# Loading queries and keys by group instead of by batch in an attention plus gated-MLP kernel

## Chip, cores and metric

One core of one Trainium2 chip. The time is the device time of one execution in microseconds; the median over several runs counts.

## The reference

Eight batches, 12 heads, 448 tokens, head dimension 64, all inputs float32. Attention with RMS-normed queries and keys is followed by a gated MLP with a spatial (token) projection. Cut to what matters:

```python
def rmsnorm(x, g):
    return x / np.sqrt(np.mean(x * x, axis=-1, keepdims=True) + 1e-06) * g

scores = matmul(rmsnorm(q, g_q), rmsnorm(k, g_k).T) / sqrt(64)
x = softmax(scores) @ v                       # 8 x 12 x 448 x 64
x = x.transpose(0, 2, 1, 3).reshape(8, 448, 768)
h = maximum(x @ w_in, 0)                      # 768 -> 1024
u, v = h[..., :512], h[..., 512:]
v = (v - mean(v)) / sqrt(var(v) + 1e-06)
v = einsum('ts,bsd->btd', w_spatial, v) + b_spatial[None, :, None]
out = (u * v) @ w_out                         # 512 -> 768
```

## The kernel before, in words

The work is cut into 24 **groups** of four heads: batch b holds groups 3b, 3b+1 and 3b+2, and group g of a batch takes heads g, g+3, g+6 and g+9. A group is handled as two pairs of heads, 128 partitions wide. For each group the kernel prepares q and k: squares (`squares`, on GpSimd, called POOL, or on ScalarE, called ACT), their sums over the head dimension (`reduce`, VectorE, called DVE), 1/rms by a logarithm and an exponential (`rstd`, ACT), the scaling to bf16 (`scaled`, POOL or DVE), and a transposition. The transposition is either done on TensorE (PE) with an identity (`transpose_pe`, followed by a copy on DVE) or by a DMA (`transpose_dma`, on the queue of SyncE, called SP); after a DMA the k side is scaled by `k_scale` on DVE (L345), tile kT from tile kr.

The scores of a group are computed in seven chunks of keys; a **pass** p is one chunk of both pairs, so group G covers passes 7G to 7G+6. Passes 0 to 19 run one at a time in the early loop (`expo` with 128x896, tile pse). From there on a **step** s covers passes 2s and 2s+1 with one exponential of 128x1792 (L372, tile et from tile pss); steps run from S0 = 10 to 83. When a group's exponentials are there, `weigh` multiplies them on PE with ones (the softmax sums) and with v (L394), `recip` turns the sums into reciprocals on ACT (L400, L401) and `xt_store` multiplies on DVE (L408). After a batch's three groups, `gated` queues that batch's MLP in pieces that `fill` hands to PE between the steps.

Every engine takes its instructions in the order of the program, which is written out by hand: `early(p)` lists what else is issued in pass p, and the tables EVEN, ODD and FIRST give the step in which a group's squares (sq), sums (red), rstd, scaling (sc), DMA transposition (tr), PE transposition (turn) and k scaling (ks) are issued, as offsets to the group's own place or, for the first groups, as absolute steps. Within a step `prep` sorts them by ORDER; `flush()` issues the output stores that the step before has left. `v_step` says when the parts of the next v are issued on POOL's queue, and the MLP's weights are issued there too (`load_w_in`, `load_w_sp`, `load_w_out`). Those transfers cast float32 to bf16.

q and k come in by SP's queue. Group 0 comes in small pieces (`load_first`, shared by SP and ACT). Groups 1 and 2 come together (`load_pair`: five heads from 1 and five from 7, k first). From batch 1 on, `load_part` brings one quarter of a batch's q or k (six heads, 384 or 288 KB) into one of two buffers, `qb0` and `qb1`. Batch 1 is issued at once, the others at the steps named first_q; a batch's load waits until the buffer's last batch has been scaled, and `qb1` takes the memory of the early tiles. The lines that issue v of batch 0 and order it behind group 1's scaled k are:

```python
        elif p == 3:
            rstd(1)
            scaled(1, 0, eng=dve)
            scaled(1, 1, eng=dve)
            after((1, 1))
            load_v(0, range(4))
```

Here `after` is a one-element copy on POOL that reads the scaled k of group 1.

Of the kernel before, what the change touches and what calls it, by code (L numbers as in the profile page):

```python
# [10 lines left out]
FP = mybir.dt.float32  # L11
BF = mybir.dt.bfloat16
# [7 lines left out]
def kernel(  # L20
# [21 lines left out]
    B, H, S, D = q.shape  # L42
    DM, DF = moe_w_in.shape
    DH = DF // 2
    P = 128
    NG = 3
    NCH = 7
# [8 lines left out]
    early_pools = ctx.enter_context(ExitStack())  # L56
    early_sb = ctx.enter_context(ExitStack())
    first = early_sb.enter_context(tc.tile_pool(name="first", bufs=1, side="right"))
    ps_e = early_pools.enter_context(tc.tile_pool(name="ps_e", bufs=2, space=PSUM, side="right"))
    ps_w = ctx.enter_context(tc.tile_pool(name="ps_w", bufs=4, space=PSUM))  # L60
    qb_pools = [ctx.enter_context(tc.tile_pool(name="qb0", bufs=1))]
# [12 lines left out]
    def lo_hi(x):  # L74
        lo = x[:, 0:256, :].rearrange("h (p c) d -> p h (c d)", c=4)
        hi = x[:, 256:S, :].rearrange("h (p c) d -> p h (c d)", c=3)
        return lo, hi
# [2 lines left out]
    k_g = [k[b].rearrange("(l g) s d -> g l s d", g=NG) for b in range(B)]  # L80
    raw = {}

    def load_pair(i):

        lo, hi = lo_hi((q, k)[i][0])
        t = first.tile([P, 5, NCH, D], FP, name=f"pair{i}")
        tv = t.rearrange("p h c d -> p h (c d)")
        for g in range(1, NG):
            raw[g, i] = t[:, g - 1:g + 3:NG]
        sync.dma_start(out=tv[0:64, :, 0:256], in_=lo[:, 1:6])  # L90
        sync.dma_start(out=tv[64:128, :, 0:192], in_=hi[:, 1:6])
        sync.dma_start(out=tv[64:128, :, 192:448], in_=lo[:, 7:12])
        sync.dma_start(out=tv[0:64, :, 256:448], in_=hi[:, 7:12])

    qbs = {}

# [39 lines left out]
    act.preload_act_table_set("natural_log_exp_and_others")  # L136
    load_first(0, 1, sync)
    load_first(1, 1, act)
    load_pair(1)
    load_pair(0)  # L140
    for n in range(8):
        load_part(1, *divmod(n, 4))


    ident = const.tile([P, P], BF)
# [262 lines left out]
        dve.tensor_tensor(out=xts[b][:, 2 * g + half, :], in0=pst.pop((G, half))[:, 0:S], in1=rec[G],  # L408
                          op=ALU.mult)

    def attend(G):
        for part in (-1, 0, 1):
            weigh(G, part)
            if part < 0:
                recip(G)
        for half in (0, 1):
            xt_store(G, half)

    def attend_late(G, i):

        if i < 3:
            weigh(G, i - 1)
        if i == 1:
            recip(G)
        if i > 1:
            xt_store(G, i - 2)

# [170 lines left out]
    S0 = 10  # L600


    squares(0, 0, 0, eng=act)
    squares(0, 1, 0)
    reduce(0, 0, 0)
    reduce(0, 1, 0)
    squares(0, 0, 1, eng=act)
# [17 lines left out]
        psp[p] = ps_e.tile([P, 2, 512], FP, name="pse")  # L625
        scores(psp[p], p)

    def after(key):

        t = st_pool.tile([1, 1], BF, name="one")  # L630
        pool.tensor_copy(out=t, in_=nrm[key][0:1, 0, 0, 0:1])


    def early(p):
        if p == 0:
            squares(1, 1)
            squares(2, 1)
            transpose_first(0, 1, dve)
            transpose_first(1, 1, dve)
        elif p == 1:  # L640
            squares(1, 0, eng=act)
        elif p == 2:
            reduce(1, 1)
            reduce(1, 0)
        elif p == 3:
            rstd(1)
            scaled(1, 0, eng=dve)
            scaled(1, 1, eng=dve)
            after((1, 1))
            load_v(0, range(4))  # L650
        elif p == 4:
            squares(2, 0, eng=act)
        elif p == 6:
            reduce(2, 1)
            reduce(2, 0)
        elif p == 8:
            rstd(2)
            scaled(2, 0, eng=dve)
            scaled(2, 1)
            squares(3, 0)  # L660
            squares(3, 1)
            load_w_in(1)
        elif p == 14:
            reduce(3, 0)
            reduce(3, 1)
        elif p == 16:
            rstd(3)
            scaled(3, 0, eng=dve)
            scaled(3, 1)
            squares(4, 0)  # L670
            squares(4, 1)
            load_w_in(0)
        elif p == 19:
            reduce(4, 0)
        if 10 <= p <= 13:
            attend_late(0, p - 10)
        if 15 <= p <= 18:
            attend_late(1, p - 15)
        if p in (0, 1, 2, 3, 4, 7, 8, 9, 14):
            dummies(6)  # L680

    TURN = {5: (1, 0), 6: (1, 1), 11: (2, 0), 12: (2, 1), 18: (3, 0), 19: (3, 1)}
    pass_scores(0)
    for p in range(2 * S0):
        expo(psp[p], p, 1)
        if p in TURN:
            transpose_pe(*TURN[p], dve)
        if p + 1 < 2 * S0:
            pass_scores(p + 1)
        early(p)  # L690
# [2 lines left out]

    EVEN = {"sq": (-11, -8), "red": (-9, -7), "rstd": (-6,), "sc": (-6, -5), "tr": (-5, -4), "ks": (-1,)}
    ODD = {"sq": (-9, -7), "red": (-6, -5), "rstd": (-3,), "sc": (-3, -2), "tr": (-2, -1), "ks": (2,)}
    FIRST = {4: {"red": (None, 10), "rstd": (11,), "sc": (11, 11), "turn": (12, 13)},
             5: {"sq": (11, 12), "red": (12, 13), "rstd": (14,), "sc": (14, 14), "turn": (15, 16)},
             6: {"sq": (14, 14), "red": (15, 16), "rstd": (17,), "sc": (17, 18), "tr": (18, 18), "ks": (20,)},
             7: {"sq": (16, 17), "red": (17, 18), "rstd": (19,), "sc": (19, 20), "tr": (20, 20), "ks": (23,)},
             8: {"sq": (18, 20), "red": (19, 21)},  # L700
             9: {"sq": (21, 23), "red": (22, 24)}}
    todo = {}
    for m in range(2, NGT // 2):
        for G, form in ((2 * m, EVEN), (2 * m + 1, ODD)):
            plan = {what: tuple(7 * m + o for o in os) for what, os in form.items()}
            if G in FIRST:
                plan = dict(plan if G > 7 else {}, **FIRST[G])
            for what, os in plan.items():
                for i, s in enumerate(os):
                    if s is not None:  # L710
                        todo.setdefault(s, []).append((what, G, i))
    for b in range(2, B):
        first_q = {2: S0, 3: 16}.get(b, (21 * b - 36) // 2)
        for n in range(4):
            todo.setdefault(first_q + n // 2, []).append(("ld", NG * b, n))
            todo.setdefault(first_q + 2 + (n if b % 2 == 0 and b > 2 else n // 2), []).append(("ld", NG * b, n + 4))

    ORDER = ("red", "rstd", "sc", "sq", "turn", "tr", "ks", "ld")

    def prep(s, early_act):  # L720
        for what, G, i in sorted(todo.get(s, ()), key=lambda x: (ORDER.index(x[0]), x[1:])):
            if (what == "rstd") != early_act:
                continue
            if what == "ld":
                load_part(G // NG, *divmod(i, 4))
            elif what == "turn":
                transpose_pe(G, i, dve)
            elif what == "sq":
                squares(G, i, eng=act if (G, i) in ((6, 1), (7, 1)) else None)
            elif what == "red":  # L730
                reduce(G, i)
            elif what == "rstd":
                rstd(G)
            elif what == "sc":
                scaled(G, i, eng=dve if (G, i) in ((4, 0), (5, 0)) else None)
            elif what == "tr":
                transpose_dma(G, i)
            elif what == "ks":
                k_scale(G)
# [5 lines left out]
    v_step = {}  # L745
    for s, b in gate_step.items():
        if b + 2 < B:
            v_step.update({s + 6 + i: (b + 2, [i]) for i in range(4)})
    busy = {attend_step(G) for G in range(NGT)}
    early_pools.close()  # L750
    early_sb.close()
    qb_pools.append(ctx.enter_context(tc.tile_pool(name="qb1", bufs=1, side="right", reuse_waits="tile")))
    ps_sc = ctx.enter_context(tc.tile_pool(name="ps_sc", bufs=1, space=PSUM, side="right", reuse_waits="tile"))
    pss = ps_sc.tile([P, 4, 512], FP, name="pss")
    rate = 0.0
    for s in range(S0, NST):
        scores(pss[:, 0:2], 2 * s)
        scores(pss[:, 2:4], 2 * s + 1)
        prep(s, True)
        expo(pss, 2 * s, 2)  # L760
        prep(s, False)
        flush()
        if s in v_step:
            load_v(*v_step[s])
        if s == 11:
            load_v(1, range(4))
        if s == 13:
            load_w_sp()
        if s == 21:
            load_w_out()  # L770
        if s in gate_step:
            b = gate_step[s]
            gated(b)
            nxt = min(x for x in list(gate_step) + [NST] if x > s)
            n = sum(1 for x in range(s, nxt - 1) if x not in busy)
            rate = sum(w[0] for w in work) / (n + 0.5)
        if s in busy:
            attend([G for G in range(NGT) if attend_step(G) == s][0])
            quota[0] = 0
        else:  # L780
            quota[0] = 1
            fill(rate)
# [9 lines left out]
    n = 0  # L792
# [35 lines left out]
```

## Time and profile before

| what | value |
|---|---|
| runs | 324.6, 325.19, 326.21 us; median 325.19 |
| profiled execution | 324.6 us, span of the instructions 322.8 us |
| PE matmul busy | 274.9 us (85% of the span) |
| ACT busy | 213.6 us (66%) |
| DVE busy | 199.0 us (62%) |
| POOL busy | 195.7 us (61%) |
| moved by DMA | 50.44 MB, mean 156 GB/s |
| mean granted TensorE clock | 0.963 |

A busy share is an average over stages with different limits, so the page's row of 40 slices and the waits of one stretch say more than the totals. A wait is listed as the engine and tile that waited, what released it, the total in us, how often, and the longest. In the timeline a line has its start, its duration, the engine, the line of the kernel, the operation with its tiles, how many instructions it merges, and in brackets the idle time before it with what ended it. PEld is the loading of PE's weights; SPq and POOLq are DMA issues on those queues.

### The profile page before, as it was taken

Reading aid. Unit: us, or ns where it says so; the run is one execution under the profiler, and the core shown is the slowest. Engines: PE = TensorE matmul, PEld = TensorE weight load, DVE = VectorE, ACT = ScalarE, POOL = GpSimd, SP = SyncE. Lnnn points to the kernel's source line nnn. Section 1 sums busy time; section 2 is a strip of 40 time slices with the busy share of each in tenths; the row PEclk is TensorE's granted clock in tenths of the full one; section 3 lists DMA queues with packets and bytes.
Section 4 is the critical chain, followed back from the end, with each engine's and each line's share of the span. In section 5 each row is a group of like instructions: output and inputs, shape, how many; then the busy total and the mean of one; then the engine's idle time right before and its main releaser. Section 6 shows DMA issues by size and latency. Waiting matters only on the chain.

```text
span 322.8 us, 6428 instructions
## 1 busy us (share of the span) xinstructions
PE 274.9 (85%) x2543; PEld 129.7 (40%) x2553; DVE 199.0 (62%) x342; ACT 213.6 (66%) x279; POOL 195.7 (61%) x175
## 2 busy tenths in 40 slices
PE   8528286979891999997999999979999999999994
PEld 8314132434440444443443444434443443444552
DVE  3737047498652759667676685686768754845552
ACT  2448157778880688776877878857786886674421
POOL 3215709985995669956986699559866960300300
PEclk9978778999998799999999999999999999999999
DMA  5999995968799999999999999998944296132156
GB/s 142 209 202 201 205 215 106 137 92 169 119 203 156 186 227 168 200 206 200 160 209 179 157 178 267 197 190 138 220 60 84 27 169 151 27 97 51 25 148 171
DMA packets 79744, 50.44 MB, mean 156 GB/s; under 512 B 42657, under 2 KB 76066, under 8 KB 79714
## 3 DMA queue, kind: packets, MB, share of 16 engines
q1 hardware_dynamic: 63922, 41.33, 67.4%
q0 software_dynamic: 15216, 8.27, 22.1%
q8 instruction: 20, 0.33, 0.5%
q10 hardware_dynamic: 576, 0.43, 0.5%
q14 instruction: 10, 0.08, 0.1%
HBM read 39.01 MB, written 11.01 MB: 155 GB/s over the span
## 4 chain that ended last, share of the span: by engine, by line
PE 41%; ACT 9%; DVE 8%; POOL 6%; DMA 6%; issue 2%; POOLq 0%; DVEq 0%; ACTq 0%
PE ps L547 9%; PE ps L473 8%; PE ps L513 7%; PE ps L394 6%; PE pss L365 6%; ACT et L372 6%; DMA w_out<-in_moe_w_out_dram 4%; PE ps L503 4%; DVE ms L256 3%; POOL sqt L248 2%; POOL vn L495 2%; DMA qT<-n 2%; DVE xt L408 1%; DVE s L481 1%; DVE osb L450 1%
## 5 line engine op out<-in xcount | busy, mean ns | idle before, releaser
L372 ACT ACTIVATE et<-pss 128x1792 bf16<-128x1792 f32 x74 | 122.9, 1661 | 46.5 <-PE pss L365 45.0
L256 DVE TENSOR_REDUCE ms<-sqt 128x14 f32<-128x896 f32 x46 | 49.3, 1075 | 21.8 <-POOL sqt L248 17.2
L408 DVE TENSOR_TENSOR xt<-ps,rc 128x448 bf16<-128x448 f32 x48 | 27.9, 619 | 43.8 <-ACT rc L401 43.1
L365 PE MATMUL pss<-qT,kT 64*128 64x448 bf16 x254 | 38.4, 360 | 17.4 <-DVE kT L345 9.1
L394 PE MATMUL ps<-et,vt 128*32 128x448 bf16 x768 | 43.7, 362 | 7.8 <-DMA vt<-in_v_dram 6.1
L547 PE MATMUL ps<-w_out,gt 128*128 128x384 bf16 (+1 forms) x256 | 48.6, 332 | 1.7 <-ACT rs L265 0.5
L473 PE MATMUL ps<-w_in_v,xt 128*128 128x512 bf16 (+1 forms) x182 | 47.0, 390 | 0.4
L275 POOL TENSOR_TENSOR n<-qb,rs 128x896 bf16<-128x896 f32 x18 | 30.5, 1694 | 24.8 <-ACT rs L265 24.7
L275 POOL TENSOR_TENSOR n<-kb,rs 128x896 bf16<-128x896 f32 x21 | 36.9, 1756 | 10.7 <-issue 9.9
L503 PE MATMUL ps<-xt,w_in_u 128*128 128x448 bf16 x192 | 40.1, 353 | 0.8 <-ACT vs L442 0.8
L248 POOL TENSOR_TENSOR sqt<-qb 128x896 f32<-128x896 f32 x21 | 36.1, 1719 | 0.0
L547 PEld LDWEIGHTS <-gt 128*128 128x128 bf16 (+1 forms) x256 | 24.6, 102 | 20.9 <-issue 7.3
L248 POOL TENSOR_TENSOR sqt<-kb 128x896 f32<-128x896 f32 x19 | 31.8, 1681 | 0.0
L394 PEld LDWEIGHTS <-vt 128*32 128x32 bf16 x768 | 21.2, 99 | 25.6 <-issue 9.0
L491 POOL TENSOR_SCALAR nm<-mv 128x4 f32<-128x4 f32 x8 | 1.8, 221 | 48.1 <-DVE mv L482 48.1
L365 PEld LDWEIGHTS <-kT 64*128 64x128 bf16 x276 | 10.8, 94 | 48.3 <-issue 28.9
L450 DVE COPY osb<-ps 128x384 f32<-128x384 f32 (+1 forms) x45 | 24.1, 555 | 9.6 <-PE ps L547 8.9
L495 POOL TENSOR_SCALAR vn<-vs,nm,rv 128x512 bf16<-128x512 bf16 (+1 forms) x32 | 24.2, 767 | 6.7 <-ACT rv L490 4.2
L513 PE MATMUL ps<-w_spT,vn 128*128 128x448 bf16 (+1 forms) x128 | 27.2, 353 | 0.1
L473 PEld LDWEIGHTS <-xt 128*128 128x128 bf16 (+1 forms) x192 | 18.2, 102 | 19.7 <-issue 5.5
L345 DVE TENSOR_SCALAR_CACHE_REDUCE kT<-kr,g_col 128x896 bf16<-128x896 bf16 x18 | 20.4, 1136 | 8.9 <-DMA kr<-n 8.9
L503 PEld LDWEIGHTS <-w_in_u 128*128 128x128 bf16 x192 | 17.3, 98 | 20.8 <-issue 7.1
(88 smaller groups left out, 336.6 us busy)
## 6 DMA issues: line engine op xcount, KB each, us to landing
out_dram<-osb SPq DMA_DIRECT2D x55, 192.0 KB, 4.3
qb<-in_q_dram SPq DMA_DIRECT2D x14, 384.0 KB, 7.0
kb<-in_k_dram SPq DMA_DIRECT2D x14, 384.0 KB, 8.7
qb<-in_q_dram SPq DMA_DIRECT2D x14, 288.0 KB, 8.3
kb<-in_k_dram SPq DMA_DIRECT2D x14, 288.0 KB, 9.6
vt<-in_v_dram POOLq DMA_DIRECT2D x16, 192.0 KB, 5.7
vt<-in_v_dram POOLq DMA_DIRECT2D x16, 144.0 KB, 5.6
w_in_v<-in_moe_w_in_dram POOLq DMA_DIRECT2D x4, 192.0 KB, 12.8
```

Of the source, the lines that this page charges most:

```text
L248: pool.tensor_tensor(out=t, in0=x, in1=x, op=ALU.mult)
L256: dve.tensor_reduce(out=sqs[gk][:, key[1], :], in_=sqt.pop(key).rearrange("p h c d -> p (h c) d"), axis=AX.X, op=ALU.add)
L275: (eng or pool).tensor_tensor(out=t.rearrange("p c h d -> p h c d"), in0=raw[key], in1=rst[gk][:, key[1], :].rearrange("p (h c) -> p h c", ...
L365: pe.matmul(out=ps[:, h, 0:S], lhsT=kT[r, c0:c0 + 128], rhs=qT[r, :], start=True, stop=True, tile_position=(64 * h, 0))
L372: act.activation(out=ets[s][:, 2 * a:2 * a + 2 * m, :], in_=ps[:, 0:2 * m, 0:S], func=AF.Exp, bias=0.0, scale=1.0)
L394: pe.matmul(out=ps[32 * l:32 * l + 32, 0:S], lhsT=w, rhs=et_of(G, 3 if r == 3 else r + 4 * y, h), start=(r == 0), stop=(r == 3), tile_posi ...
L408: dve.tensor_tensor(out=xts[b][:, 2 * g + half, :], in0=pst.pop((G, half))[:, 0:S], in1=rec[G], op=ALU.mult)
L473: pe.matmul(out=ps[0:m, :], lhsT=xts[b][:, j, t0:t0 + m], rhs=w_in_v[:, j, :], start=(j == 0), stop=(j == 5), tile_position=(0, 0))
L495: pool.tensor_scalar(out=vn_t[b % 2][0:m, c, :], in0=vs[b][c][0:m, :], scalar1=nms[b][0:m, c:c + 1], scalar2=rvs[b][0:m, c:c + 1], op0=ALU ...
L503: pe.matmul(out=ps[:, 0:S], lhsT=w_in_u[:, j, 128 * f:128 * f + 128], rhs=xts[b][:, j, :], start=(j == 0), stop=(j == 5))
L513: pe.matmul(out=ps[:, 0:S], lhsT=vn_t[b % 2][0:kp, c, 128 * f:128 * f + 128], rhs=w_spT[0:kp, c, :], start=(c == 0), stop=(c == NT - 1))
L547: pe.matmul(out=ps[o:o + m, 0:384], lhsT=gts[b][f][:, t0:t0 + m], rhs=w_out[:, f, r], start=(f == 0), stop=(f == 3), tile_position=(0, o))
```

## The change

Groups 1 to 8 (batches 0, 1 and 2) are loaded one group at a time into a pool of three buffers each for q and k; from batch 3 on the loads stay by batch. k of group 1 is issued on POOL's queue. The issues of v and of the MLP's weights move to other passes and steps, and the helper `after` goes. Groups 4 and 5 are transposed by DMA instead of on PE, group 3's transposition on PE moves behind the early loop, and the squares and scalings that ACT and DVE did for groups 4 to 7 go to POOL. `attend_late` is replaced by an `attend` that takes parts. The step tables of groups 4 to 9, first_q and v_step are changed, and the early memory is released at step 24 instead of step 10. `flush()`, `recip` and everything in the MLP stay.

The short description of the changed version reads: output stores issued in the next step, behind that step's loads and transposes; reciprocal computed in place; that of the version before: first batch loaded in three transfer sets, others a batch at a time. The stores by `flush()` in the next step and the reciprocal in place (`recip`) are in both.

```diff
+    qk_pool = early_sb.enter_context(tc.tile_pool(name="qk", bufs=3, side="right"))
...
-    def load_pair(i):
...
+    def load(G, i, eng=sync):
+        b, g = divmod(G, NG)
+        lo, hi = lo_hi((q_g, k_g)[i][b][g])
+        t = qk_pool.tile([P, 2, NCH, D], FP, name="kf" if i else "qf")
         tv = t.rearrange("p h c d -> p h (c d)")
...
+        raw[G, i] = t
+        eng.dma_start(out=tv[0:64, :, 0:256], in_=lo[:, 0:2])
+        eng.dma_start(out=tv[64:128, :, 0:192], in_=hi[:, 0:2])
+        eng.dma_start(out=tv[64:128, :, 192:448], in_=lo[:, 2:4])
+        eng.dma_start(out=tv[0:64, :, 256:448], in_=hi[:, 2:4])
...
-    load_pair(1)
-    load_pair(0)
-    for n in range(8):
-        load_part(1, *divmod(n, 4))
+    load(1, 0)
+    load(2, 0)
+    load(2, 1)
+    load(3, 0)
+    load(3, 1)
...
     squares(0, 1, 0)
+    load(1, 1, pool)
...
         if p == 0:
             squares(1, 1)
+            load_v(0, range(4))
+            load_w_in(1)
             squares(2, 1)
+            load_w_in(0)
...
-            after((1, 1))
-            load_v(0, range(4))
...
-        elif p == 8:
+        elif p == 9:
             rstd(2)
             scaled(2, 0, eng=dve)
             scaled(2, 1)
             squares(3, 0)
             squares(3, 1)
-            load_w_in(1)
+            load_v(1, range(4))
...
-        elif p == 16:
+        elif p == 15:
             rstd(3)
             scaled(3, 0, eng=dve)
             scaled(3, 1)
             squares(4, 0)
             squares(4, 1)
-            load_w_in(0)
+            load_w_sp()
...
-        if p in (0, 1, 2, 3, 4, 7, 8, 9, 14):
+        if p not in (0, 6, 10, 11, 12, 13, 16, 17, 18):
             dummies(6)
-    TURN = {5: (1, 0), 6: (1, 1), 11: (2, 0), 12: (2, 1), 18: (3, 0), 19: (3, 1)}
...
+        if p in (6, 13):
+            transpose_pe(p // NCH + 1, 0, dve)
+            transpose_pe(p // NCH + 1, 1, dve)
+        if p in (4, 5):
+            load(4, p - 4)
+        if p in (10, 11):
+            load(5, p - 10)
+        if p in (16, 17):
+            load(6, p - 16)
...
-    FIRST = {4: {"red": (None, 10), "rstd": (11,), "sc": (11, 11), "turn": (12, 13)},
-             5: {"sq": (11, 12), "red": (12, 13), "rstd": (14,), "sc": (14, 14), "turn": (15, 16)},
-             6: {"sq": (14, 14), "red": (15, 16), "rstd": (17,), "sc": (17, 18), "tr": (18, 18), "ks": (20,)},
-             7: {"sq": (16, 17), "red": (17, 18), "rstd": (19,), "sc": (19, 20), "tr": (20, 20), "ks": (23,)},
-             8: {"sq": (18, 20), "red": (19, 21)},
-             9: {"sq": (21, 23), "red": (22, 24)}}
+    FIRST = {4: {"red": (None, 10), "rstd": (11,), "sc": (11, 11), "tr": (11, 11), "ks": (13,)},
+             5: {"sq": (10, 11), "red": (11, 12), "rstd": (13,), "sc": (13, 14), "tr": (14, 14), "ks": (16,)},
+             6: {"sq": (13, 14), "red": (14, 15), "rstd": (16,), "sc": (16, 17), "tr": (17, 17), "ks": (20,)},
+             7: {"ldg": (12, 12), "sq": (15, 17), "red": (17, 18), "rstd": (19,), "sc": (19, 19), "tr": (19, 20),
+                 "ks": (23,)},
+             8: {"ldg": (15, 15), "sq": (18, 20)}}
...
-    for b in range(2, B):
-        first_q = {2: S0, 3: 16}.get(b, (21 * b - 36) // 2)
+    SC8 = 23
+    for b in range(3, B):
+        first_q = max(15 if b == 3 else SC8 + 1, (21 * b - 38) // 2)
...
-                squares(G, i, eng=act if (G, i) in ((6, 1), (7, 1)) else None)
+                squares(G, i)
...
-                scaled(G, i, eng=dve if (G, i) in ((4, 0), (5, 0)) else None)
+                scaled(G, i)
...
-            v_step.update({s + 6 + i: (b + 2, [i]) for i in range(4)})
+            v_step.update({s + 4 + i: (b + 2, [i]) for i in range(4)})
...
+    transpose_pe(3, 0, dve)
+    transpose_pe(3, 1, dve)
     rate = 0.0
     for s in range(S0, NST):
+        if s == SC8 + 1:
+            early_sb.close()
...
-        if s == 11:
-            load_v(1, range(4))
-        if s == 13:
-            load_w_sp()
-        if s == 21:
+        if s == 18:
             load_w_out()
```

## The prediction

> **What bounds the kernel now.** I read the page's 40 slices, then the list of waits, then the timeline of the exponentials (L372, one per step), because every group must pass through them in order.
>
> ```profile
> PE   8528286979891999997999999979999999999994
> ACT  2448157778880688776877878857786886674421
> DMA  5999995968799999999999999998944296132156
> GB/s 142 209 202 201 205 215 106 137 92 169 119 203 156 186 227 168 200 206 200 160 209 179 157 178 267 197 190 138 220 60 84 27 169 151 27 97 51 25 148 171
> ```
>
> One slice is 8.07 us. From slice 13 (105 us) PE is at 9 almost throughout. Before that PE and ACT have holes while DMA is full in slices 1 to 5 (about 205 GB/s) and only partly used in 6 to 10. So the front is a matter of what arrives when; the rest is PE's.
>
> ```profile
> ACT et L372 <- PE ps L394: 9.9, 1, 9.9
> ACT sqt L246 <- DMA pair<-in_q_dram: 6.0, 1, 6.0
> DVE kT L345 <- DMA kr<-n: 8.9, 2, 7.8
> PE pss L365 <- DVE kT L345: 9.1, 2, 7.2
> ```
>
> The last two lines are one event. So there are three losses, each placed by the timeline (start, duration, what; the idle time before it in brackets):
>
> ```profile
> 20.48 0.95 ACT L246 ACTIVATE sqt<-pair 128x896 f32<-128x896 f32 x1 [6.00 <-DMA pair<-in_q_dram]
> ...
> 25.83 2.74 POOL L130 DMA_DIRECT2D vt<-in_v_dram  x4
> ...
> 43.60 4.16 ACT L372 ACTIVATE et<-pse 128x896 bf16<-128x896 f32 x5 [9.87 <-PE ps L394]
> ```
> ```profile
> 91.05 3.56 SPq L339 DMA_TRANSPOSE kr<-n  x1
> ...
> 103.21 1.15 DVE L345 TENSOR_SCALAR_CACHE_REDUCE kT<-kr,g_col 128x896 bf16<-128x896 bf16 x1 [7.79 <-DMA kr<-n]
> ...
> 105.02 1.66 ACT L372 ACTIVATE et<-pss 128x1792 bf16<-128x1792 f32 x1 [7.91 <-PE pss L365]
> ```
>
> (1) q of groups 1 and 2 lands at 20.5. (2) v of batch 0, issued at 25.8, lands by 39.7; PE's weighing and behind it the exponential of pass 12 wait. (3) Group 7's transposed k (issued at 91.0, landing 12.1 us later) holds step 24 for 7.9 us. After that the steps are periodic: step 35 is at 138.60 and step 56, two batches on, at 204.57; steps 36 and 57 at 141.68 and 207.65. The same 65.97 us repeats, so no transfer but the order of the work sets the pace. What the change does before step 24 to 29 goes straight to the end; afterwards I expect nothing.
>
> **What the Trainium skill says.** "DMA: Bandwidth & Descriptors", Issuing engines are not separate DMA queues, with Queues, rings and completion order: queues share the same 16 engines, taking turns by packet. The trace agrees: with SP's queue full, v took about 9 to 11.7 us to land after issue, with SP's queue empty (at 60 us) about 4.6. "SBUF — State Buffer", Who interferes with whom: a VectorE operation with two SBUF inputs keeps GpSimd's reads out. POOL's scaling takes 2.5 to 2.6 us where DVE scales at the same time (48.35, 30.35) and 1.69 otherwise.
>
> **The change, part by part.** G is a group, p a pass of the early loop (0 to 19), s a step (10 to 83).
>
> *Not changed:* the stores in `flush()` and the in-place reciprocal that the change's short description names stand in both kernels (L401, rc<-rc x24). They cost nothing here.
>
> *Loads of groups 1 to 8.* Eight batch loads and two five-head pairs (24 DMAs) become 64 DMAs of 128 or 96 KB, 60 on SP and 4 (k of group 1) on POOL. 0.46 MB of double loading goes. SP issues one in 0.62 to 0.65 us: 459 KB per 2.6 us, a ceiling of 176 GB/s for SP alone. Order now follows need: q1, q2, k2, q3, k3. First pieces (0.92 MB) end at about 7.6; q1 at 205 GB/s lands near 10.6; k1, issued 8.2 to 11 on POOL and sharing with q2, near 15.5 (k lands at 14.09 today). A plain float32 load on POOL's queue is not in the trace. The nearest rows are SP's pair, 5.0 us after issue at best, and v in traffic, 9.2: the last piece lands between 15.5 and 20, and at 20 the first gain below all but vanishes; I take 15.5 since only 0.92 MB share the engines then. Then square 1.7 on POOL (17.2), reduction 1.1, rstd 0.6, two scalings of 1.1 on DVE, transposes and copies about 2: first exponential of group 1 at 23.3 instead of 28.09, **4.8 earlier**.
>
> *v of batch 0* is issued after that square, 17 to 20 instead of 25.8 to 28.6. With the same 9 to 11.7 us it lands at 29 to 31 instead of 39.7. But w_in is now issued behind it on POOL's queue, and in the built program a POOL transfer waits for the one eight before it: w_in_u waits for v to land, and behind w_in_u stands group 2's scaling on POOL. So POOL's n of group 2 is ready near 33 to 35, pass 14's exponential near 36.5 instead of 45.4: **8.9 earlier**.
>
> *Given back until s = 10.* v of batch 1 waits in the same way for w_in_v (lands near 40), ahead of group 3's scaling: 1.7 (to 41.7), the square of group 4 another 1.7, reduction 1.1 (44.5). On DVE this reduction now stands before the copies of group 3's transposes, which moved from p = 18, 19 to after the loop: copies 1.3, scores 0.5. Step 10 starts at 46.5 to 48.3 instead of 52.69: **4.4 to 6.2 earlier**.
>
> *Groups 4 and 5 by DMA instead of PE.* Off PE: 28 transposes, some 3.5 us (0.93 for seven). Off DVE: four copies, 2.6 us, for two k scalings of 1.14. PE's share lay beside idle PE in s = 12 to 16. In place comes a wait: SP's two transposes of group 4 follow POOL's scalings (51 to 54), land in 3 to 6 us (2.9 to 3.1 at 81 to 84 us, median of all 5.4 and 5.7; in the traffic at 91 us it was 12.1, which would cost 6 more here) at 57 to 60. DVE's k scaling at s = 13 waits, and queued behind it are batch 0's statistics and PSUM evictions. Step 14 at about 61 instead of 66.9: 6 earlier.
>
> *Work moved to POOL:* squares (6,1), (7,1) from ACT and scalings (4,0), (5,0) from DVE, 4 x 1.68 = 6.7 us, plus 2.8 for k1's issue. POOL is idle for 8.3 and 9.9 us up to 48 today, so it fits, but it is why groups 4 to 7 arrive just in time. 12 more dummies on PE (0.5 us per six) run beside ACT.
>
> *Steps 14 to 24.* Batch 3 now starts at s = 15 without waiting for a buffer (today SP waits from 41 to 70.7); its k stands behind group 6's transposes and ahead of group 7's, as today. Bytes due before group 7's k, counted as written: first 0.92, groups 1 to 8 7.34, batch 3 2.75, v of three batches 2.07, w_in 1.57, w_sp 0.40, w_out 0.79, eight transposes 1.84: 17.7 MB, at 205 GB/s 86 us, from 3 us on. I add 7 us for stretches where SP waits for POOL to free one of three buffers: lands near 96, plus k scaling 1.1, scores and start 1.7. Step 24 at 98.8 instead of 105.0: **6.2 earlier**. Bounds: 91 (step 10 plus 14 steps at the later pace of 3.14) and 112 (below).
>
> *Later:* v is issued two steps earlier and batches 5 to 7 one step earlier. Two q parts (0.67 MB, 3.3 us) now precede a k transpose; its consumer follows some 10 us after landing (group 17: issued 200.1, needed near 215). Zero, at most 3 us.
>
> Sum: profiled execution 324.6 (span 322.8 and 1.8 around it) - 6.2 = 318.4; the median was 0.6 above that execution: **319.0**.
>
> **Rivals.**
>
> *The small loads are too slow (slower).* SP's issue ceiling of 176 GB/s, with only eight of 112 KB in flight: if one takes 5.5 us to complete, 0.9 MB per 5.5 us is 163 GB/s. At 165 the 17.7 MB take 107 us, group 7's k lands at 110, step 24 at 112.8: +7.8, about **333**. It decides from 177 GB/s down (17.7 MB over the 100 us until today's 103.2). For it: POOL's and SP's waits are all in order. Against: POOL's transfers add to SP's, and slices 1 to 5 show over 200. Chance 0.36 with every result over 0.5% slower, from 327 on.
>
> *Only the place of the wait changes (same).* DMA is the front's limit in both: group 7's k lands near 102, **325**. For it: the same bytes are due, and the transposes of groups 7 and 8 took 9.8 to 12.1 us in traffic. Against: slices 6 to 10 show free DMA today. Chance 0.10.
>
> *No wait takes their place (much faster).* Step 24 at 91, **311**. Against: POOL's load. Part of the 0.54 for faster.
>
> **Numbers.** 0.5% (1.6 us) is about what measurement can tell from no change. Faster 0.54, same 0.10, slower 0.36. My case's own range is 314 to 322; with half of the slower case and the gain in full, 311 to 331.
>
> **What would show it.** Right: q wait of 6.0 and the 9.9 behind L394 gone or under 3; first exponential of group 1 near 23, step 10 near 47, step 14 near 61, step 24 near 99; a DVE wait for kr of group 4; intervals after step 29 as before. Wrong: step 10 at 52 or later (POOL held at w_in_u), under 177 GB/s up to 100 us with SP always issuing, or a changed pace after step 29.

## The result, and the profile after

The changed kernel takes 316.39 us (median of 4 runs, 315.18 to 317.86) against 325.67 for the kernel before in the same comparison: ratio 0.972, 95% interval 0.967 to 0.978. The profiled execution took 317.15 us (span 315.3), 7.45 less than the one before. In all experiments below a ratio is to the kernel before run on the same chip (325.7 to 327.0); times of different comparisons are compared through these ratios. Medians are of all executions while ratios leave out those that ran slow, so the two can differ by a few thousandths.

The same four rows of the page's 40 slices (one slice is now 7.88 us):

```profile
PE   8758759996498999979999899979999999999994
ACT  2767868884367887766776887747877786764421
DMA  5999996899988999999879999999435592132156
GB/s 142 207 186 236 230 239 130 157 195 158 215 163 127 220 163 292 193 194 193 202 131 190 178 200 226 204 163 208 113 49 93 55 229 46 27 100 52 26 152 175
```

The front's DMA stretch is denser (236, 230, 239 in slices 3 to 5, where it was about 205), and the hole in ACT that ran from 34 to 44 us is gone. A hole remains in PE and ACT in slices 9 and 10 (counted from 0), that is at 71 to 87 us. The list of waits (us in total, times, longest) names both:

```profile
DVE kT L346 <- DMA kr<-n: 7.6, 3, 6.9
POOL sqt L249 <- DMA kf<-in_k_dram: 5.0, 1, 5.0
ACT et L373 <- PE ps L395: 1.7, 2, 0.9
POOL w_in_u L198 <- DMA vt<-in_v_dram: 1.3, 1, 1.3
```

ACT's 6.0 us for q has become POOL's 5.0 for k of group 1. The 9.9 us behind the weighing are two waits of under 1 us. The wait for a transposed k is there again, 6.9 us long. The timelines of POOL, DVE and ACT place them:

```profile
15.17 1.68 POOL L249 TENSOR_TENSOR sqt<-kf 128x896 f32<-128x896 f32 x1 [4.97 <-DMA kf<-in_k_dram]
16.80 2.67 POOL L130 DMA_DIRECT2D vt<-in_v_dram  x4
...
24.55 2.54 ACT L373 ACTIVATE et<-pse 128x896 bf16<-128x896 f32 x3 [2.71 <-PE pse L366]
...
44.05 1.66 ACT L373 ACTIVATE et<-pss 128x1792 bf16<-128x1792 f32 x1 [2.06 <-PE pss L366]
...
81.86 1.15 DVE L346 TENSOR_SCALAR_CACHE_REDUCE kT<-kr,g_col 128x896 bf16<-128x896 bf16 x1 [6.92 <-DMA kr<-n]
84.04 1.66 ACT L373 ACTIVATE et<-pss 128x1792 bf16<-128x1792 f32 x1 [7.84 <-PE pss L366]
...
95.82 1.66 ACT L373 ACTIVATE et<-pss 128x1792 bf16<-128x1792 f32 x1 [1.52 <-PE pss L366]
```

v is issued 9.0 us earlier, step 10 starts 8.6 us earlier (44.05 against 52.69), and step 21 waits 7.8 us, where it waited 1.0 before; step 24 waits 1.5, where it waited 7.9. Start of the exponential of a step, in us:

| step | 10 | 14 | 17 | 20 | 21 | 24 | 29 | 38 | 39 | 59 | 60 |
|---|---|---|---|---|---|---|---|---|---|---|---|
| before | 52.69 | 66.90 | 76.90 | 86.39 | 89.06 | 105.02 | 122.04 | 150.41 | 153.30 | 216.39 | 219.28 |
| after | 44.05 | 55.15 | 63.86 | 74.53 | 84.04 | 95.82 | 110.87 | 139.69 | 144.27 | 207.36 | 211.88 |
| earlier by | 8.6 | 11.8 | 13.0 | 11.9 | 5.0 | 9.2 | 11.2 | 10.7 | 9.0 | 9.0 | 7.4 |

So there are three things to explain: which part of the change gave the 8.6 us; why group 6's transposed k is late; and why 11.2 us at step 29 are 7.5 at the end, two losses of about 1.65 us among them, between steps 38 and 39 and between 59 and 60.

### The profile page after: what moved, and what is told of

The parts are those of the page before. It is cut to its first block, busy times and chain, and to the rows that moved or that the text cites. A ratio compares the mean times of both kernels' runs of the same rounds, so it can differ in the third digit from the quotient of the medians.

```text
span 315.3 us, 6473 instructions
## 1 busy us (share of the span) xinstructions
PE 277.5 (88%) x2527; PEld 129.5 (41%) x2537; DVE 197.4 (63%) x340; ACT 212.2 (67%) x277; POOL 203.6 (65%) x182
## 4 chain that ended last, share of the span: by engine, by line
PE 40%; DMA 15%; DVE 13%; POOL 12%; ACT 9%; SPq 5%; issue 5%; POOLq 0%; DVEq 0%
PE ps L540 8%; PE ps L466 8%; PE ps L506 7%; PE ps L395 6%; PE pss L366 6%; ACT et L373 5%; POOL sqt L249 5%; PE ps L496 4%; DMA kb<-in_k_dram 4%; POOL n L276 4%; DMA qf<-in_q_dram 4%; DVE ms L257 3%; DMA kr<-n 3%; DMA kf<-in_k_dram 3%; DVE s L474 2%
## 5 line engine op out<-in xcount | busy, mean ns | idle before, releaser
L373 ACT ACTIVATE et<-pss 128x1792 bf16<-128x1792 f32 x74 | 122.8, 1660 | 49.6 <-PE pss L366 45.9
L540 PE MATMUL ps<-w_out,gt 128*128 128x384 bf16 (+1 forms) x256 | 49.3, 335 | 1.2 <-ACT rs L266 0.5
L466 PE MATMUL ps<-w_in_v,xt 128*128 128x512 bf16 (+1 forms) x182 | 45.4, 381 | 0.4
L496 PE MATMUL ps<-xt,w_in_u 128*128 128x448 bf16 x192 | 41.9, 365 | 0.8 <-ACT vs L435 0.8
L276 POOL TENSOR_TENSOR n<-qb,rs 128x896 bf16<-128x896 f32 x15 | 25.4, 1693 | 25.7 <-ACT rs L266 25.7
L249 POOL TENSOR_TENSOR sqt<-kb 128x896 f32<-128x896 f32 x15 | 25.1, 1682 | 9.9 <-DVE gt L510 9.8
L506 PE MATMUL ps<-w_spT,vn 128*128 128x448 bf16 (+1 forms) x128 | 28.7, 367 | 0.1
L346 DVE TENSOR_SCALAR_CACHE_REDUCE kT<-kr,g_col 128x896 bf16<-128x896 bf16 x20 | 22.7, 1135 | 7.6 <-DMA kr<-n 7.6
L276 POOL TENSOR_TENSOR n<-kb,rs 128x896 bf16<-128x896 f32 x15 | 25.4, 1693 | 0.1
L249 POOL TENSOR_TENSOR sqt<-qb 128x896 f32<-128x896 f32 x15 | 25.2, 1679 | 0.0
## 6 DMA issues: line engine op xcount, KB each, us to landing
kb<-in_k_dram SPq DMA_DIRECT2D x10, 288.0 KB, 10.7
```

The lines of the kernel that those rows point to most:

```text
L249: pool.tensor_tensor(out=t, in0=x, in1=x, op=ALU.mult)
L276: (eng or pool).tensor_tensor(out=t.rearrange("p c h d -> p h c d"), in0=raw[key], in1=rst[gk][:, key[1], :].rearrange("p (h c) -> p h c", ...
L373: act.activation(out=ets[s][:, 2 * a:2 * a + 2 * m, :], in_=ps[:, 0:2 * m, 0:S], func=AF.Exp, bias=0.0, scale=1.0)
L466: pe.matmul(out=ps[0:m, :], lhsT=xts[b][:, j, t0:t0 + m], rhs=w_in_v[:, j, :], start=(j == 0), stop=(j == 5), tile_position=(0, 0))
L496: pe.matmul(out=ps[:, 0:S], lhsT=w_in_u[:, j, 128 * f:128 * f + 128], rhs=xts[b][:, j, :], start=(j == 0), stop=(j == 5))
L506: pe.matmul(out=ps[:, 0:S], lhsT=vn_t[b % 2][0:kp, c, 128 * f:128 * f + 128], rhs=w_spT[0:kp, c, :], start=(c == 0), stop=(c == NT - 1))
```

## The experiments

**v earlier, alone.** The kernel before with one edit:

```diff
         if p == 0:
             squares(1, 1)
+            load_v(0, range(4))
             squares(2, 1)
...
-            after((1, 1))
-            load_v(0, range(4))
```

> The kernel before with one edit: v of batch 0 is issued at pass 0, right after the square of k of group 1, and not behind the scalings of group 1 (its one-element copy goes). Theory A (v was the front's main loss, and a front that is early stays early): v is issued near 16 to 19, lands near 27, the 9.9 us wait of pass 12 behind the weighing shrinks below 3, step 10 starts at 46 to 48 instead of 52.7, and as the release of the batch buffers moves with it, so does group 7's k: step 29 at 116 to 118, time 319 to 321. Rival B (the batch-sized loads and group 7's transposed k set the end of the front, wherever v is): step 10 is early as well, but the wait before step 24 grows from 7.9 to 12 or more, and the time stays within 1.6 us of 325.7.

Measured 317.55 us, ratio 0.970 (0.963 to 0.977): as large a gain as the whole change has, from one moved line and one dropped. The timelines of POOL and ACT:

```profile
15.24 2.74 POOL L130 DMA_DIRECT2D vt<-in_v_dram  x4
...
34.62 4.16 ACT L372 ACTIVATE et<-pse 128x896 bf16<-128x896 f32 x5 [1.61 <-PE ps L394]
...
43.70 1.66 ACT L372 ACTIVATE et<-pss 128x1792 bf16<-128x1792 f32 x1 [1.02 <-PE pss L365]
```

v took 10.5 to 14.4 us to land, longer than before, and that was soon enough. Step 10 starts at 43.70 with q and k still in pairs and group 1 as late as ever (27.36), and step 29 at 112.02. Theory A holds, and by more than it expected (step 29 at 116 to 118, time 319 to 321). In the kernel before, v was simply asked for too late.

**v late again in the changed kernel.** v moved back to pass 3, behind the scaled k of group 1:

```diff
             squares(1, 1)
-            load_v(0, range(4))
             load_w_in(1)
...
             scaled(1, 1, eng=dve)
+            after((1, 1))
+            load_v(0, range(4))
```

> The changed kernel with one edit: v of batch 0 is issued at pass 3 behind the scaled k of group 1 (with the one-element copy that the kernel before has), while w_in keeps its new place at pass 0. Theory A (v's place is worth most of the gain up to step 10): v is issued near 22 to 25, lands at 30 to 33, the exponential waits 4 to 7 us for the weighing again, step 10 starts at 48 to 51 instead of 44.05; time 318 to 322. Rival B (the small loads in order of need carry the gain, and the later v hides behind group 2): step 10 within 1.5 us of 44.05, time within 1.6 us of 316.4. Either way the wait of 6.9 us for group 6's transposed k (step 21) can take in part of the loss: if it does, step 24 is later by less than step 10 is.

Measured 328.12 us, ratio 1.003 (0.999 to 1.006): the whole gain is gone, and the wait is longer than either theory said. Its ACT timeline:

```profile
43.82 1.73 ACT L373 ACTIVATE et<-pse 128x896 bf16<-128x896 f32 x2 [14.51 <-PE ps L395]
...
56.90 1.66 ACT L373 ACTIVATE et<-pss 128x1792 bf16<-128x1792 f32 x1 [2.06 <-PE pss L366]
```

But this run does not move v alone: v now stood behind both halves of w_in on POOL's queue (v took 12.6 to 14.2 us to land). So the next run put w_in behind v again.

**v late, w_in behind it.**

```diff
             scaled(1, 1, eng=dve)
+            after((1, 1))
+            load_v(0, range(4))
...
+            load_w_in(1)
             load_v(1, range(4))
...
+            load_w_in(0)
             load_w_sp()
```

> The changed kernel with v of batch 0 issued at pass 3 behind the scaled k of group 1, and, other than in the run with v alone moved, w_in back behind it too: w_in_v at pass 9 ahead of v of batch 1, w_in_u at pass 15 ahead of w_sp. In that run v stood behind both halves of w_in on POOL's queue and the exponential waited 14.5 us. Theory A (v's own issue time decides; a v issued at 23 to 26 with little else on POOL lands at 31 to 34): the exponential waits 4 to 7 us for the weighing, step 10 starts at 47 to 50, time 318 to 322. Rival B (most of that wait was w_in ahead of v): the wait is under 3 us, step 10 by 46, time 315.5 to 318.

The wait is short (1.96 us) and step 10 early, as the rival had it. Its timelines of POOL and ACT:

```profile
21.25 2.67 POOL L130 DMA_DIRECT2D vt<-in_v_dram  x4
...
31.57 1.73 ACT L373 ACTIVATE et<-pse 128x896 bf16<-128x896 f32 x2 [1.96 <-PE ps L395]
...
43.75 1.66 ACT L373 ACTIVATE et<-pss 128x1792 bf16<-128x1792 f32 x1 [2.06 <-PE pss L366]
```

The same program line is reached 4.6 us earlier than in the kernel before (21.25 against 25.83), as group 1 is scaled earlier, and v lands in 4.4 to 6.5 us; step 10 comes at 43.75. The time does not settle it: the four runs scatter from 313.9 to 322.1 (median 319.36, ratio 0.983, 0.977 to 0.989), and the profile is that of the shortest. What the profile shows is the front. With the rest of the change in place, v issued at 21 is in time; with v issued at 15, the pairs of before do as well. **Either part of the change removes the same wait, so their gains do not add**; only v behind w_in is worse than both. Which piece of the rest does it (the small loads, their order, or what left the queues) was not taken apart.

**q ahead of k, in the kernel before.**

```diff
-    load_pair(1)
     load_pair(0)
+    load_pair(1)
```

> The kernel before with one edit: the five-head transfers of q are issued ahead of those of k, so that q of group 1 arrives first. If the 6.0 us wait for q were only a matter of order, the exponential of group 1 would start 4 to 5 us earlier than 28.1. If it is one of size (q and k of two groups, 1.1 MB each way, must both be there before the group can be scaled), the wait only goes over from ACT, which squares q, to POOL, which squares k: k lands near 20, and group 1's first exponential is at 27.5 to 30. I expect the second. The time: within 1.6 us of 325.7 by that theory, 321 to 323 by the first.

As expected, the wait only went over to POOL: its square of k waits 12.9 us, and group 1's first exponential is at 30.38. Yet the time was 321.61, ratio 0.985 (0.979 to 0.990), 4.5 us less: the time of the first theory, for a reason that neither gave. v was issued at 27.9, two us later than before, but landed in 7.4 to 7.8 us instead of 8.9 to 11.7: the next batch's loads on SP started at 35.3 instead of 31.4, after v. The exponential waited 2.77 us for the weighing and started at 40.05, 3.6 us earlier. Of these, 1.9 are v's last piece (37.67 against 39.54). The other 1.7 are the weighing behind it: it took 4.1 us in the kernel before, at half clock (36.9 to 43.8), and 2.4 here at full clock. So it is v again; that SP's later loads are the reason for its quicker landing fits the times, but no run moves them alone.

**Groups 4 and 5 transposed on PE, as before.** In the changed kernel (the two table rows are shortened; the lines that let `prep` issue "turn" come back with them):

```diff
-    4: {..., "sc": (11, 11), "tr": (11, 11), "ks": (13,)},
-    5: {..., "sc": (13, 14), "tr": (14, 14), "ks": (16,)},
+    4: {..., "sc": (11, 11), "turn": (12, 13)},
+    5: {..., "sc": (13, 14), "turn": (15, 16)},
```

> The changed kernel with one edit: q and k of groups 4 and 5 are transposed on PE, with copies by DVE, as in the kernel before, instead of by DMA; their scalings stay on POOL. Steps 10 to 17 took 24.2 us before and 19.8 after, 4.4 less. Theory A (28 transposes of about 0.13 us on PE, 3.5 us, and 1.4 us of DVE work were on the path of steps 12 to 16): step 17 comes 3 to 4 us later than 63.9. Rival B (PE and DVE had room there, and the 4.4 us come from loads that are in time): step 17 within 1 us of 63.9. In both cases the wait before step 21 ends at the same DMA, or earlier as four transposes leave SP's queue, so the time is 315.5 to 319.

312.35 us, ratio 0.957 (0.953 to 0.962), below the whole expected range: undoing this part of the change gains some 4 us more. Step 17 is at 65.51, 1.65 later than 63.86, between the theories. But step 10 was 1.7 earlier in this run, so steps 10 to 17 took 23.2 us and not 19.8, and a stretch of half clock (42.8 to 49.6) lies in them. The run below that has batch 3's loads earlier and k of group 1 on SP besides passes the same steps at full clock, in 20.6 us. That speaks for rival B: PE and DVE had room for these transposes. Step 21 is at 78.09 with a wait of 1.0 us instead of 7.8. Without the four transposes, SP's queue moves on: in the changed kernel the first transpose (issued 47.97) and the second (49.61, after POOL's scaling) stand ahead of group 7's loads (50.89 on), and those of group 5 ahead of group 8's (59.45 on). Here these loads go out from 46.22 and 54.87, and batch 3's q stands further from group 6's k (8.3 us ahead instead of 6.2). SP's timelines, of the changed kernel and of this run:

```profile
65.08 2.61 SPq L105 DMA_DIRECT2D qb<-in_q_dram  x4
67.86 3.34 SPq L340 DMA_TRANSPOSE qT<-n  x1
71.31 3.38 SPq L340 DMA_TRANSPOSE kr<-n  x1
```
```profile
61.55 2.60 SPq L105 DMA_DIRECT2D qb<-in_q_dram  x4
64.32 1.72 SPq L340 DMA_TRANSPOSE qT<-n  x1
69.82 1.22 SPq L340 DMA_TRANSPOSE kr<-n  x1
```

In the first k lands 10.5 us after its issue, in the second 5.1.

**Batch 3's loads three steps earlier** (q at steps 12 and 13, k at 14 and 15), in the changed kernel:

```diff
-        first_q = max(15 if b == 3 else SC8 + 1, (21 * b - 38) // 2)
+        first_q = max(12 if b == 3 else SC8 + 1, 12 if b == 3 else (21 * b - 38) // 2)
```

> The changed kernel with one edit: the batch loads of batch 3 are put three steps earlier (q at steps 12 and 13, k at 14 and 15), so that they stand behind group 7's loads and ahead of group 8's, and nothing but w_out and v is near group 6's transposes. Theory A (the 6.9 us wait before step 21 is the transposes sharing the DMA engines with the 1.3 MB of batch 3's q issued right ahead of them): the transposes land within 6 us of issue, the wait falls under 2, step 24 starts at 90 to 93 instead of 95.8, time 311 to 313.5. Rival B (the loads ahead of the transposes are all late, because SP's queue stood still behind the transposes of groups 4 and 5 until POOL had scaled them; the bytes are the same whatever their order): the wait stays at 5 us or more or moves to group 7's k (step 24), time within 1.6 us of 316.4.

316.40 us, ratio 0.967 (0.965 to 0.970). The wait followed the load: batch 3's q (issued from 56.98) now stands right ahead of group 5's transposes (issued 59.71, landing in 8.0 us, and 62.60, there when DVE starts at 69.86). DVE waits for the second, and step 17 for DVE (6.4 us):

```profile
69.86 1.15 DVE L346 TENSOR_SCALAR_CACHE_REDUCE kT<-kr,g_col 128x896 bf16<-128x896 bf16 x1 [6.08 <-DMA kr<-n]
...
85.26 1.15 DVE L346 TENSOR_SCALAR_CACHE_REDUCE kT<-kr,g_col 128x896 bf16<-128x896 bf16 x1 [2.82 <-DMA kr<-n]
```

Theory A is supported in part: group 6's k lands in 8.7 us instead of 10.5 (not under 6), and step 21 waits 3.1 instead of 7.8 (not under 2). The time is rival B's: the wait changes its place. The next run takes that place away, as groups 4 and 5 have no DMA transposes in it:

**Both edits together.**

> The changed kernel with two edits: groups 4 and 5 transposed on PE (measured alone: 312.35), and batch 3's loads three steps earlier. In the first alone step 24 still waits 2.9 us and steps 21 to 22 take 6.2 us. Theory A (both are transposes in the company of batch 3's loads): steps 10 to 29 at the later pace of 3.14 us, step 29 at 102 to 105 instead of 107.7, time 307 to 310. Rival B (with PE transposes SP's queue is free early anyway, and the earlier batch loads only push group 8's back): within 1.6 us of 312.4.

309.28 us (308.67 to 309.56), ratio 0.946 (0.943 to 0.948): the best version, clear of the changed kernel's interval, and the time is inside theory A's range, with step 29 (105.18) just behind its 102 to 105. Group 6's k lands in 6.7 us. The same DVE line:

```profile
77.36 1.15 DVE L346 TENSOR_SCALAR_CACHE_REDUCE kT<-kr,g_col 128x896 bf16<-128x896 bf16 x1 [0.74 <-DMA kr<-n]
```

**w_out at step 21, as before,** in the changed kernel:

```diff
-        if s == 18:
+        if s == 21:
             load_w_out()
```

> The changed kernel with one edit: w_out (768 KB in one transfer on POOL's queue) is issued at step 21, as in the kernel before, not at 18. In the changed kernel it goes out at 73.56, while group 6's two transposes (issued 67.86 and 71.31) are under way, and from 76 to 80 us the DMA moves only 124 GB/s; in the run with batch 3's loads earlier it goes out at 77.79, after them, and they landed sooner. Theory A (w_out beside the transposes is what makes them land after 10.5 us): the transposes land within 6 us, the rate at 76 to 80 stays over 160 GB/s, the wait before step 21 is under 3 us, step 22 at 85 to 87 instead of 89.3, time 312 to 314.5 unless group 7 then waits. Rival B (batch 3's q, issued right ahead of the transposes, is what holds them): the wait is 5 us or more again, time within 1.6 us of 316.4.

320.38 us, ratio 0.984 (0.978 to 0.990), slower than the changed kernel, if barely clear of its interval. Group 6's k lands after 10.7 us as it did, and the wait stays; w_out, now issued at 91.44, is late itself. From DVE's and PE's timelines:

```profile
82.31 1.15 DVE L346 TENSOR_SCALAR_CACHE_REDUCE kT<-kr,g_col 128x896 bf16<-128x896 bf16 x1 [6.82 <-DMA kr<-n]
...
98.80 0.48 PE L540 MATMUL ps<-w_out,gt 128*64 128x384 bf16 x1 [3.56 <-DMA w_out<-in_moe_w_out_dram]
```

Theory A falls here: with batch 3's q right ahead, w_out was not what held the transposes. Step 25 waits 5.25 us for w_out in this run, and step 29 comes at 114.42, 3.6 us later than in the changed kernel: in these two profiles that is what its earlier issue is worth.

**k of group 1 on SP's queue,** in the changed kernel and, besides, in the best version:

```diff
     load(1, 0)
+    load(1, 1)
...
-    load(1, 1, pool)
```

> The changed kernel with one edit: k of group 1 is loaded on SP's queue, right behind q of group 1, instead of on POOL's. Theory A (POOL's queue was a detour: issue from 7.7, landing at 15.2): k is issued 8.2 to 10.2 on SP and lands near 13.5, POOL's square of it starts 1.5 us earlier, v and w_in with it, and POOL has 2.7 us less to issue; group 1's first exponential at 22.5 to 23.5 instead of 24.55; time 314.5 to 316. Rival B (q and k of groups 2 and 3 come 2.6 us later, and nothing in the end follows group 1): step 10 within 1 us of 44.05, time within 1.6 us of 316.4.

314.50 us, ratio 0.964 (0.958 to 0.970): k landed by 12.94, step 10 came at 42.88, and in the profile step 21 waits 9.2 us instead of 7.8. The time is within theory A's range, the interval overlaps that of the changed kernel: no difference is shown.

> The changed kernel with three edits: groups 4 and 5 transposed on PE, batch 3's loads three steps earlier (both together measured 309.28), and k of group 1 on SP's queue (alone: step 10 1.2 us earlier, time 314.5 against 316.4). Theory A (the front now follows group 1 without a later DMA wait that takes it in): step 10 at 41 to 42.5, step 29 at 103.5 to 104.5, time 307.5 to 308.8. Rival B (steps 19 to 24 wait for batch-sized loads and take it in): step 29 within 0.5 us of 105.2, time 308.9 to 309.8.

311.11 us, ratio 0.955 (0.950 to 0.959): slower than without it (0.943 to 0.948), outside both ranges. The profile is that of the longest run of six (315.64), and there group 6's k lands 12 us after an issue at 71.68 and step 21 waits 11.2 us. So even with batch 3's q long landed (63.6) the transposes can be late. w_out went out at 72.00, 0.3 us after that k, so the next run moves it away.

> The run with groups 4 and 5 on PE, batch 3's loads earlier and k of group 1 on SP (311.11; its profile waits 10.3 us for group 6's transposed k, issued 0.3 us before w_out), with w_out at step 21 besides. Theory A (w_out beside the transposes): that wait is under 2 us, step 29 at 102 to 105, time 306.5 to 309. Rival B (it is chance or batch 3's loads): a wait of 5 us or more before step 21, time 309.5 to 312.5.

311.58 us (306.86 to 313.32), ratio 0.948 (0.938 to 0.958): the interval covers both theories. In the profile, of the shortest run, w_out goes out at 81.95, group 6's k lands in 7.0 us instead of 12.0, and DVE waits for it for 3.5 us, between the two theories. These are one profile each, and v's transfers, too, stood 1 us further back, so w_out's part is suggested here, not shown.

**No dummy transposes in the early passes.**

```diff
         if p not in (0, 6, 10, 11, 12, 13, 16, 17, 18):
-            dummies(6)
+            pass
```

> The changed kernel without the six dummy transposes on PE in 11 of the 20 early passes (66 instructions, 5.5 us of PE). Theory A (they lie beside the exponentials and cost nothing; their count does not matter): step 10 within 1 us of 44.05, time within 1.6 us of 316.4. Rival B (dummies stand ahead of scores in PE's queue and some of them are on the path): step 10 earlier by 1 to 3 us, time 313.5 to 315.5. Rival C (they decide when the half-speed spells of PE's clock come): the spells near 140 and 208 us, each of which costs one step 1.65 us, come in other steps or are fewer, and the mean clock rises from 0.954.

317.35 us, ratio 0.968 (0.962 to 0.974), step 10 at 44.39: leaving out 66 PE instructions gains nothing. The clock went the other way than rival C said: 0.928 to 0.941 in the four executions, where the changed kernel has 0.953 to 0.956. In the profiles, 23.9 us before step 13 run at half clock, against 10.2; step 20 comes 2.5 us later (77.05), and the wait before step 21 takes most of that in (6.2 us instead of 7.8). The two late stretches of half clock come all the same (140.8 to 144.2 and 209.0 to 212.4 us).

**The two late losses** need no run of their own. Two stretches around step 39 (us, busy time and count of PE, PEld, DVE, ACT, POOL, then granted clock, DMA share, GB/s), first of the changed kernel, then of the one with v earlier alone:

```profile
141.00:146.00 5.00, 5.00 (x54) 2.28 (x56) 1.18 (x2) 2.95 (x6) 4.97 (x5) 0.79 1.46 206
```
```profile
141.00:146.00 5.00, 5.00 (x69) 2.29 (x66) 1.18 (x2) 4.60 (x7) 4.98 (x5) 1.00 0.97 154
```

PE is busy for all of the 5 us in both, with 54 instructions at a clock of 0.79 against 69 at 1.00. Steps 38 to 39 take 4.58 us in the first and 2.89 in the second. The loss goes with the clock, not with the changed order: the run with groups 4 and 5 on PE has the changed kernel's later order and takes 2.89 and 2.88 us for the two places; the run with q first has the later order of before and takes 4.57 and 4.53, and that with v early takes 4.57 for steps 59 to 60.

What stands before it is the same in both orders: at step 38 PE idles for 1.9 us, where it waits for DVE's scaled k. The changed kernel, then the kernel before:

```profile
139.29 0.36 PE L366 MATMUL pss<-qT,kT 64*128 64x448 bf16 x2 [1.88 <-DVE kT L346]
```
```profile
150.01 0.36 PE L365 MATMUL pss<-qT,kT 64*128 64x448 bf16 x2 [1.89 <-DVE kT L345]
```

The traces also show when the clock can change. In each of the fourteen profiles the stretches of half clock start whole multiples of 3.41 us apart and, but for the one that runs into the end, last 3.41 us or a multiple of it. So a grid of marks, 3.41 us apart, runs through every execution; its offset from the start of the span differs between profiles, from 0.8 to 3.3 us. Two stretches between marks around step 38, with the same columns as above, of the changed kernel and of the kernel before:

```profile
136.29:139.71 3.42, 1.54 (x10) 0.50 (x8) 3.35 (x7) 0.91 (x4) 1.98 (x4) 1.00 1.15 193
139.71:143.12 3.41, 3.41 (x11) 1.39 (x10) 0.80 (x2) 2.51 (x4) 3.41 (x4) 0.50 1.22 190
```
```profile
146.17:149.58 3.41, 1.95 (x11) 0.76 (x9) 3.31 (x7) 1.73 (x4) 1.15 (x3) 1.00 1.17 191
149.58:153.00 3.42, 2.99 (x19) 1.40 (x19) 2.13 (x5) 2.53 (x4) 3.42 (x4) 1.00 1.18 211
```

In the changed kernel the idle time lies wholly between two marks: PE is busy for 45% of that stretch, and the next 3.41 us run at half clock. In the kernel before a mark at 149.58 cuts it: the two stretches are busy for 57% and 88%, and the clock stays at 1.00. The same idle time comes at steps 38 and 59 of all fourteen profiles. In 15 of these 28 places it lies between two marks, and in 14 of the 15 half clock follows (in the other it begins within 0.02 us of a mark). In the 13 places where a mark cuts it, each stretch is busy for at least 49%, and half clock never follows. So the two late losses are a matter of where the marks fall in an execution. The Trainium skill, "TensorE: Matmul & The Clock Gate", What's actually happening, says that the clock falls to half after an idle window of about 3.4 us, and that this window runs freely, so that it matters where in it the work lands. The half clock, the length and the free running agree with the traces; but the window need not be idle: one with 1.9 us of idle time in it was enough here.

## Why the prediction was right, point by point

- *Verdict and size.* 319.0 was forecast and 316.39 measured; step 24 gained 9.2 us, not 6.2, and 1.7 of that surplus was lost again by the end (7.45 in the profile against 6.2). That the sum came so near is in part luck: step 14 was 5.9 us ahead of its forecast (55.15 against 61), and group 6's wait, which the working did not have, took half of that back by step 24.
- *k of group 1.* Said to land at 15.5, landed by 15.17. Group 1's first exponential came at 24.55, not 23.3: one of the two scalings on DVE took 2.57 us, not 1.1. The working found no plain float32 load on POOL's queue in the trace; there were two, of 0.5 KB, landing in 3.1 and 3.9 us, and the four pieces of k took 3.4 to 5.4.
- *v of batch 0.* The issue was right (17 to 20 forecast, 16.80 to 19.5 measured). The term "9 to 11.7 us" to land was too long: it took 4.8 to 7.7. SP's loads that were issued ahead of v had landed by 18.8; in the kernel before such loads were still landing until 34.0. So POOL's wait at w_in_u was 1.33 us, the block at v of batch 1 did not happen, pass 14's exponential came at 34.46, not 36.5 (before, it was at 45.22, not 45.4), and step 10 at 44.05, not 46.5 to 48.3.
- *The attribution was wrong.* The working gave q's part 4.8 and v's 8.9 in one chain. The runs show that v's earlier issue alone is sufficient (step 10 at 43.70), and that its new place is not needed where the rest of the change is in (43.75). Group 1's earlier start is not needed for it: where v alone is early, group 1 starts at 27.36.
- *Groups 4 and 5 by DMA.* I priced in a wait of 3 to 6 us at step 13; it was 0.31, as the transposes landed in 2.9 to 3.0 us. What I did not price is the queue: SP's loads stood behind these transposes until POOL had scaled. I put "7 us for stretches where SP waits for POOL" on the byte sum and so expected the loss at group 7's k. It came three steps earlier, at group 6's.
- *The Trainium skill, "DMA: Bandwidth & Descriptors", Issuing engines are not separate DMA queues.* Sharing of the engines fits group 6: its k lands in 10.5 us behind 1.3 MB of batch 3's q, group 4's in 2.9 with nothing near. Batch 3's k, v and w_out are issued around it, too, and the runs do not part their shares.
- *Later: zero, at most 3.* The profile lost 3.7 us after step 29 (11.2 to 7.5); 3.3 are the two stretches of half clock. The idle PE ahead of them is in both orders; whether the clock falls depends on where the marks of its grid lie.
- *Rivals.* The slow one needed under 177 GB/s: from 20 to 45 us the DMA moved 224 to 246, with SP's pieces 0.65 us apart where it had a free buffer. "Only the place of the wait changes" was half true: a wait of 6.9 replaced one of 7.8, but from a front 12 us earlier.

What stays open: why group 6's k took 12.0 us in one run of the version with k on SP, with the same instructions ahead of it as in the version without k on SP, where it took 6.7. Batch 3's q does not explain it. w_out may: it went out 0.3 us behind that k, 4.6 us behind it where k took 6.7, and 11 us behind it where k took 7.0. But with batch 3's q right ahead it made no difference (10.5 and 10.7 us).

## What to carry to other kernels

When several loads feed one wait, ask first which of them was requested last, and move that request alone; here reordering everything else removed the same wait a second time, and so added nothing. A DMA that waits for an engine holds back all loads queued behind it, so its price is read from those, not from its own landing. And before explaining a loss in a steady stretch by the order of work, compare the instructions per microsecond and the granted clock there, and look at where the idle time lies between the clock's marks.

## What the runs showed of the hardware that was not expected

- PE's granted clock drops to 0.50 for 3.4, 6.8, 10.2 or 13.7 us at a time, and in a stretch where PE is the bound one such drop of 3.4 us cost 1.65 us. The same idle time of 1.9 us ahead of it brought the drop in 14 of 15 places where it lay between two marks of a 3.41-us grid, and in none of 13 where a mark cut it. Leaving out 66 dummy instructions gave a lower mean clock (0.933 against 0.954 in the profiles), not a higher one.
- A DMA transpose of 128x896 landed after 2.9 to 3.0 us with little else on the engines, and after 10.5, 10.7 and 12 us in the traffic at 71 us. From 76 to 80 us in the changed kernel the DMA moved only 124 GB/s while their busy share was 2.21, the highest of the 4-us stretches from 64 to 92.
- On DVE a scaling with two SBUF inputs took 1.96 or 2.57 us instead of 1.09 in stretches in which POOL squared or issued transfers; in the version with k on SP one took 1.09 while POOL issued w_in. Which of POOL's actions does it was not separated.
